# One activation for a gate and its sigmoid, a later place for a tile's split, and a ninth output buffer

## The chip, the cores and the metric

The kernel runs on one core of one Trainium2 chip. The time is device microseconds of one execution. The median of three runs of the kernel before is 1108.38 us (1107.98 to 1109.35).

## The reference

Attention with a sigmoid in place of a softmax feeds a gated layer with RMS norm, whose output feeds a second block that has no nonlinearity of its own. All is float32.

```
scores = q @ k.T / sqrt(64) - log(448)            # 4 batches, 12 heads, 448 tokens
x      = sigmoid(scores) @ v                      # 1792 tokens x 768
xn     = x / sqrt(mean(x*x) + 1e-6) * rms_g
g      = xn @ w_gate                              # 768 -> 1536
val    = xn @ w_val
y      = (g * sigmoid(g) * val) @ w_out           # 1536 -> 768
out    = ((y @ w1) * (y @ w2)) @ w3 @ w_out2      # 768 -> 1024 -> 768
```

## The kernel before

Everything is kept transposed: features on the 128 partitions, the 448 tokens of a batch along the row. A matmul in full precision is made of three fast ones (`mm3`, L296 to L298): each operand is split into a rounded high part and the rest. For weights the split is made by ScalarE or GpSimd (high part, L126 or L128) and GpSimd (rest, L129); for activations by `split2`: ScalarE writes the high part (L312), VectorE the rest (L315). Weights arrive as pairs of 32-bit words and VectorE builds float32 of them in five operations (`to_float`, L106 to L119). So VectorE works as a decoder of weights through the first quarter of the kernel, and its other work stands in the same queue between the decoding steps.

The program runs in stages. First comes attention for batches 0 and 1: twelve `visit`s, one for each pair of heads. In a visit TensorE makes the scores of one pair (L377, L389) and the product with v of the pair before (`attend`, L403, L407), and ScalarE copies that product out of its one accumulator buffer (`take_out`, L427) into a tile `xr`. These tiles are few (`A1`, `xr=8`); a tile comes free when `load_x` (L469, VectorE) has multiplied it by the norm's factor, which for batch 0 can happen only after that batch's norm (L445 to L456). Beside the last visits `split_x` makes the operands of the next stage.

Then come three pairs of `w3o_group`s (w3 times w_out2, L339 to L341, copied out at L343), with the norm and the splits of batch 1 between them on VectorE, and then the gated layer for batches 0 and 1: for each of twelve tiles m and each batch b a gate group and a value group of 18 fast matmuls each (`a_group`). For m below 6 a pair of `w3o_group`s follows each m up to m = 4; from m = 6 on the attention of batches 2 and 3 runs beside the gated tiles, a visit at a time. The second product (`b_group`) follows, and then the same work for batches 2 and 3, where each seven products replace eight (`winograd`, `a_winograd`). The last third is the second block.

In `a_group` the gate's accumulator is read twice: by the sigmoid on ScalarE (L591) and by the product with it on VectorE (L592). The value's accumulator is read by VectorE (L596), and then comes the split of the finished tile (L312, L315). Accumulators `psm` are three in a ring, shared by the gated groups, the w3 groups, the norm and half of the scores. For batch 1 and m below 6 the two accumulators of the attention scores (`sc`) are used, under the name `psa`.

A scheduler lays out each engine's queue from the program; each engine works through its queue in order, so an instruction that waits holds up all behind it.

Of the kernel before, what the change touches and what calls it, by code (L numbers as in the profile page):

```python
# [11 lines left out]
AF = mybir.ActivationFunctionType  # L12
ALU = mybir.AluOpType
# [6 lines left out]
KF1 = FF1 // P  # L20
# [23 lines left out]
def fused_kernel(ctx: ExitStack, tc: tile.TileContext, qkv, wg, wv, wo, w1, w2, w3, wo2, gam, out):  # L44
    nc = tc.nc

    def pool(name, side=None, space=None):
        kw = {}
        if side:
            kw["side"] = side  # L50
        if space is not None:
            kw["space"] = space
        return tc.alloc_tile_pool(name=name, bufs=1, **kw)
# [29 lines left out]
    def scratch(name):  # L83
        return scr.tile([P, S], F32, tag="s", bufs=6, name=name)
# [215 lines left out]
    def accumulate(tiles, xts, ps=None):  # L300
        ps = psm()[:, :S] if ps is None else ps
        n = len(xts)
        j = 0
        for t, kt in tiles:
            for kw in range(kt):
                mm3(ps, t, kw, xts[j], j == 0, j == n - 1)
                j += 1
        return ps

    def split2(dst, src, scalar=True):  # L310
        if scalar:
            nc.scalar.activation(dst[:, 0, :], src, AF.Copy)  # L312
        else:
            nc.gpsimd.tensor_copy(out=dst[:, 0, :], in_=src)
        nc.vector.tensor_tensor(out=dst[:, 1, :], in0=src, in1=dst[:, 0, :], op=ALU.subtract)  # L315
# [30 lines left out]

    A1 = dict(raw=3, a=5, al=2, xr=8, wd=2)
    A2 = dict(raw=2, a=3, al=2, xr=2)  # L350
    att = {"bufs": A1, "pool": pool("att1", "left")}

# [3 lines left out]
    raw, probs, av, acc = {}, {}, {}, {}  # L356
# [119 lines left out]
    def split_x(b, k):  # L476

        if k < KD:
            ready.append(load_x(b, k))
        if k:  # L480
            t = acts["x", b, k - 1] = x_tile("x", b)
            split2(t, ready.pop(0), b == 1)
# [7 lines left out]
    def right_blocks(k, b11, b12, b21, b22):  # L490

        tt = nc.vector.tensor_tensor

        def put(j, bl, src):
            t = acts["w", j, k] = right_tile(f"w{j}", bl)
            split2(t, src)

        t1 = scratch("t1")
        put(0, 0, b11)
        tt(out=t1, in0=b12, in1=b11, op=ALU.subtract)  # L500
        put(5, 1, t1)
        put(2, 0, b21)
        tt(out=t1, in0=b22, in1=t1, op=ALU.subtract)
        put(1, 2, t1)
        tt(out=b12, in0=b22, in1=b12, op=ALU.subtract)
        put(3, 2, b12)
        tt(out=b21, in0=b21, in1=t1, op=ALU.subtract)
        put(4, 2, b21)
        put(6, 1, b22)
# [47 lines left out]
    def a_winograd(m):  # L557
        def done(b, g, v):
            s = scratch("s")
            nc.scalar.activation(s, g, AF.Sigmoid)  # L560
            nc.vector.tensor_tensor(out=s, in0=g, in1=s, op=ALU.mult)
            nc.vector.tensor_tensor(out=s, in0=s, in1=v, op=ALU.mult)  # L562
            acts["h", b, m] = t = h_tile("hm", m)
            split2(t, s)

        winograd(i_a2, m, done)
# [10 lines left out]
    def h_tile(name, m):  # L577
        return pools[f"h{int(m >= KF1 // 2)}"].tile([P, 2, S], F32R, tag="h", bufs=KF1, name=name)
# [3 lines left out]
    def a_group(m, b, which):  # L582
        t = W.get(i_a[m][which])
        ps = None
        if b and m < KF1 // 2:

            ps = ps_sc.tile([P, 2, 512], F32, tag="sc", bufs=2, name="psa")[:, 0, :S]
        ps = accumulate([(t, 6)], [acts["x", b, k] for k in range(KD)], ps)
        if which == 0:
            s = scratch("s")  # L590
            nc.scalar.activation(s, ps, AF.Sigmoid)  # L591
            nc.vector.tensor_tensor(out=s, in0=ps, in1=s, op=ALU.mult)  # L592
            half[m, b] = s
        else:
            s = half.pop((m, b))
            nc.vector.tensor_tensor(out=s, in0=ps, in1=s, op=ALU.mult)  # L596
            t = h_tile("hm", m)
            split2(t, s)
            acts["h", b, m] = t

    def b_group(g, m, b):
        t = [(W.get(i), 6) for i in (i_b2 if g else i_b)[m]]
        ps = accumulate(t, [acts["h", b, k] for k in range(KF1)])
        y = scratch("yf")
        nc.scalar.activation(y, ps, AF.Copy)
        d = yd[g, b, m] = dram.tile([P, S], F32, name=f"y{g}{b}{m}")
        nc.sync.dma_start(out=d, in_=y)
# [8 lines left out]
    def a_units():  # L616
        for m in range(KF1):
            for b in range(2):
                for which in range(2):
                    yield 3.4, (lambda m=m, b=b, w=which: a_group(m, b, w)), i_a[m][which]  # L620

    def b_units(g):
        for m in range(KD):
            for b in range(2):
                yield 6.8, (lambda m=m, b=b: b_group(g, m, b)), (i_b2 if g else i_b)[m][1]
# [62 lines left out]
    a = list(a_units())  # L688
# [118 lines left out]
```

## Time and profile before

| | |
|---|---|
| median of 3 runs | 1108.38 us (1107.98 to 1109.35) |
| profiled execution, its own time | 1100.06 us |
| its span, from the first to the last instruction | 1098.0 us |
| TensorE matmul busy | 1078.6 us (98%) |
| VectorE busy | 801.1 us (73%) |
| ScalarE busy | 387.8 us (35%) |
| GpSimd busy | 476.2 us (43%) |
| mean granted TensorE clock | 0.994 |

PE is TensorE, DVE VectorE, ACT ScalarE, POOL GpSimd. Busy time is summed over the whole span, and so says nothing of a single stage; the rows further down are from single stages.

### The profile page before, as it was taken

To read this page: it belongs to the slowest core of one execution; us is meant where nothing else is said; L and a number is where in the kernel's file an instruction comes from. 1 tells how busy PE (TensorE), PEld (TensorE's weight loads), DVE (VectorE), ACT (ScalarE), POOL (GpSimd) and SP (SyncE) were. 2 spreads that over 40 slices of the span, in tenths; PEclk is the share of its full clock that TensorE was granted. 3 is DMA by queue.
4 is the path that set the end of the run, shared out by engine and by line. 5 is a ranking of instruction groups with operands and counts; after the bars stand their busy time and mean duration, and the time that the engine had idled before them with its cause. 6 is when DMAs were issued, how large, how long until landed. Compare 5 with 4: busy or idle time off the path is not lost.

```text
span 1098.0 us, 14086 instructions
## 1 busy us (share of the span) xinstructions
PE 1078.6 (98%) x5152; PEld 897.2 (82%) x5152; DVE 801.1 (73%) x1054; ACT 387.8 (35%) x707; POOL 476.2 (43%) x382
## 2 busy tenths in 40 slices
PE   9989999998999999999999999999999999999998
PEld 4337899996766676799989898999999999999997
DVE  5988998898446678679889999677787544777500
ACT  5664201111344433214544443133433244333221
POOL 2655443443233323342666554223665424656320
PEclk9989999998999999999999999999999999999999
DMA  7733455557345367653311113666311253210131
GB/s 253 263 131 127 148 172 154 161 194 271 122 158 169 112 244 262 237 214 107 103 59 58 58 58 101 235 248 223 104 59 58 68 166 122 77 58 29 47 100 51
DMA packets 60980, 153.22 MB, mean 140 GB/s; under 512 B 5872, under 2 KB 32624, under 8 KB 60912
## 3 DMA queue, kind: packets, MB, share of 16 engines
q1 hardware_dynamic: 60912, 152.33, 41.2%
q8 instruction: 41, 0.67, 0.2%
q14 instruction: 27, 0.22, 0.1%
HBM read 114.95 MB, written 37.36 MB: 139 GB/s over the span
## 4 chain that ended last, share of the span: by engine, by line
PE 72%; DVE 2%; ACT 1%; DMA 1%; POOL 0%; issue 0%; SPq 0%; DVEq 0%; POOLq 0%; ACTq 0%
PE psm L296 12%; PE psm L297 11%; PE psm L298 11%; PE w L296 10%; PE w L297 10%; PE w L298 10%; PE av L407 3%; PE sc L389 2%; PE psm L377 1%; PE av L403 1%; PE psm L389 1%; DMA wd<-in_wg 1%; DVE s L562 0%; POOL ws L129 0%; ACT a L394 0%; DVE wf L108 0%
## 5 line engine op out<-in xcount | busy, mean ns | idle before, releaser
L296 PE MATMUL w<-w,ws 128*128 128x448 f32 x588 | 216.8, 369 | 1.4 <-DVE c L544 1.1
L297 PE MATMUL w<-w,ws 128*128 128x448 f32 x588 | 216.2, 368 | 0.0
L298 PE MATMUL w<-w,ws 128*128 128x448 f32 x588 | 215.7, 367 | 0.0
L129 POOL TENSOR_TENSOR ws<-wf,ws 128x768 fp32r<-128x768 f32 (+1 forms) x88 | 150.7, 1713 | 139.1 <-ACT ws L126 128.4
L129 POOL TENSOR_TENSOR ws<-wd,ws 128x384 fp32r<-128x384 f32 x112 | 126.8, 1147 | 90.2 <-ACT ws L126 81.3
L129 POOL TENSOR_TENSOR ws<-s,ws 128x384 fp32r<-128x384 f32 x84 | 97.4, 1164 | 78.7 <-ACT ws L126 77.0
L128 POOL CAST ws<-wf 128x768 fp32r<-128x768 f32 (+1 forms) x52 | 47.3, 909 | 181.4 <-DVE wf L119 89.6
L296 PEld LDWEIGHTS w<-w,ws 128*128 128x128 f32 x588 | 110.3, 188 | 14.4 <-issue 3.5
L298 PEld LDWEIGHTS w<-w,ws 128*128 128x128 f32 x588 | 110.4, 188 | 10.8
L297 PEld LDWEIGHTS w<-w,ws 128*128 128x128 f32 x588 | 110.4, 188 | 10.4
L312 ACT ACTIVATE hm<-s 128x448 fp32r<-128x448 f32 x48 | 27.8, 579 | 231.6 <-DVE s L596 174.4
L296 PE MATMUL psm<-hm,ws 128*128 128x448 f32 x288 | 106.6, 370 | 0.0
L297 PE MATMUL psm<-hm,ws 128*128 128x448 f32 x288 | 105.7, 367 | 0.0
L298 PE MATMUL psm<-hm,ws 128*128 128x448 f32 x288 | 105.2, 365 | 0.0
L108 DVE TENSOR_SCALAR wf<-mag 128x768 uint32<-128x768 uint32 (+1 forms) x76 | 66.3, 873 | 36.0 <-POOL ws L129 32.2
L296 PE MATMUL psm<-x,ws 128*128 128x448 f32 x216 | 81.9, 379 | 5.6 <-ACT w3ot L343 2.9
L116 DVE SCALAR_TENSOR_TENSOR wf<-wd,wf 128x768 uint32<-128x768 uint32 (+1 forms) x76 | 85.6, 1126 | 2.3
L119 DVE SCALAR_TENSOR_TENSOR wf<-wd,wf 128x768 uint32<-128x768 uint32 (+1 forms) x76 | 78.9, 1038 | 1.5
L297 PE MATMUL psm<-x,ws 128*128 128x448 f32 x216 | 79.7, 369 | 0.0
L298 PE MATMUL psm<-x,ws 128*128 128x448 f32 x216 | 79.5, 368 | 0.0
L106 DVE TENSOR_SCALAR mag<-wd 128x768 uint32<-128x768 uint32 (+1 forms) x76 | 50.2, 660 | 33.1 <-DMA wd<-in_wo 22.8
L126 ACT ACTIVATE ws<-wd 128x384 fp32r<-128x384 f32 x112 | 54.6, 514 | 46.7 <-PE w L298 38.2
(123 smaller groups left out, 2129.3 us busy)
## 6 DMA issues: line engine op xcount, KB each, us to landing
raw<-in_qkv SPq DMA_DIRECT2D x23, 736.0 KB, 5.5
wd<-in_wo SPq DMA_DIRECT2D x20, 768.0 KB, 5.5
wd<-in_w SPq DMA_DIRECT2D x16, 768.0 KB, 5.0
wd<-w SPq DMA_DIRECT2D x32, 384.0 KB, 3.4
wd<-in_wg SPq DMA_DIRECT2D x12, 768.0 KB, 4.6
wd<-in_wv SPq DMA_DIRECT2D x12, 768.0 KB, 4.7
wd<-in_w SPq DMA_DIRECT2D x16, 512.0 KB, 4.4
w<-wf SPq DMA_DIRECT2D x16, 384.0 KB, 2.6
```

The costliest lines, as they stand in the source:

```text
L106: nc.vector.tensor_scalar(out=mag.bitcast(U32), in0=hi, scalar1=0x7FFFFFFF, scalar2=None, op0=ALU.bitwise_and)
L108: nc.vector.tensor_scalar(out=u, in0=mag.bitcast(U32), scalar1=3, scalar2=0x3FFFFFFF, op0=ALU.logical_shift_left, op1=ALU.bitwise_and,)
L116: nc.vector.scalar_tensor_tensor(out=u, in0=hi, scalar=0xC0000000, in1=u, op0=ALU.bitwise_and, op1=ALU.bitwise_or)
L119: nc.vector.scalar_tensor_tensor(out=u, in0=lo, scalar=29, in1=u, op0=ALU.logical_shift_right, op1=ALU.bitwise_or)
L126: nc.scalar.activation(t[:, 0, :w], f[:, :w], AF.Copy)
L128: nc.gpsimd.tensor_copy(out=t[:, 0, :w], in_=f[:, :w])
L129: nc.gpsimd.tensor_tensor(out=t[:, 1, :w], in0=f[:, :w], in1=t[:, 0, :w], op=ALU.subtract)
L296: nc.tensor.matmul(ps, wl, xt[:, 0, :], start=first, stop=False)
L297: nc.tensor.matmul(ps, wh, xt[:, 1, :], start=False, stop=False)
L298: nc.tensor.matmul(ps, wh, xt[:, 0, :], start=False, stop=last)
L389: nc.tensor.matmul(ps[j], r[d, k], r[d, Q0 : Q0 + S], start=True, stop=True)
L407: nc.tensor.matmul(av[p][d, :], r[:, v + j * D : v + (j + 1) * D], a[:, j, :], start=False, stop=(c == 2))
```

## The change

Three things change. In `a_winograd`, and in `a_group` for m below 6, one activation (`Silu`) computes the gate times its sigmoid; the product on VectorE falls away there, and in `a_group` the gate's accumulator has then one reader. In `a_group` the split of a finished tile is not queued at once: it is kept in a list and queued behind the next gate's activation (or at the start of the next `b_group`), and `keep_in_program_order` holds its ScalarE half at that place in the queue. And the first attention stage has nine `xr` tiles in place of eight.

```
     def split2(dst, src, scalar=True, pin=False):
         if scalar:
-            nc.scalar.activation(dst[:, 0, :], src, AF.Copy)
+            i = nc.scalar.activation(dst[:, 0, :], src, AF.Copy)
+            if pin:
+                tc.keep_in_program_order(i)
...
-    A1 = dict(raw=3, a=5, al=2, xr=8, wd=2)
+    A1 = dict(raw=3, a=5, al=2, xr=9, wd=2)
...
             s = scratch("s")
-            nc.scalar.activation(s, g, AF.Sigmoid)
-            nc.vector.tensor_tensor(out=s, in0=g, in1=s, op=ALU.mult)
+            nc.scalar.activation(s, g, AF.Silu)
             nc.vector.tensor_tensor(out=s, in0=s, in1=v, op=ALU.mult)
...
             s = scratch("s")
-            nc.scalar.activation(s, ps, AF.Sigmoid)
-            nc.vector.tensor_tensor(out=s, in0=ps, in1=s, op=ALU.mult)
+            alone = m < KF1 // 2
+            nc.scalar.activation(s, ps, AF.Silu if alone else AF.Sigmoid)
+            gated()
+            if not alone:
+                nc.vector.tensor_tensor(out=s, in0=ps, in1=s, op=ALU.mult)
             half[m, b] = s
         else:
             s = half.pop((m, b))
             nc.vector.tensor_tensor(out=s, in0=ps, in1=s, op=ALU.mult)
             t = h_tile("hm", m)
-            split2(t, s)
+            unsplit.append((t, s))
             acts["h", b, m] = t
 
+    unsplit = []
+    def gated():
+        if unsplit:
+            split2(*unsplit.pop(0), pin=True)
+
     def b_group(g, m, b):
+        gated()
```

What stands in the queues moves at the gated tiles. TensorE's queue and GpSimd's are the same in both programs, SyncE's has a store and a neighbouring load swapped at a few places, and up to the first gated tile ScalarE's and VectorE's are too, the ninth `xr` tile included: it moves no instruction. The program's lines shift by two to five (before L591, L592, L596, L312, L315, L343; after L594, L597, L601, L312, L317, L345).

The first place is ScalarE's queue at the first gated tiles. Before, from the table load for the first gate on (`s` are the gates, `hm` the high parts of the finished tiles, `w3ot` the copies of the w3 groups):

```order
L591 ACT_TABLE_LOAD
L591 ACTIVATE s_1085<-psm_1066 128x448
L312 ACTIVATE hm_1108<-s_1085 128x448
L591 ACTIVATE s_1130<-psa_1111 128x448
L312 ACTIVATE hm_1153<-s_1130 128x448
L343 ACTIVATE w3ot_1193<-psm_1156 128x384
L343 ACTIVATE w3ot_1247<-psm_1222 128x384
L591 ACTIVATE s_1281<-psm_1262 128x448
```

The same place in the changed program:

```order
L594 ACT_TABLE_LOAD
L594 ACTIVATE s_1085<-psm_1066 128x448
L594 ACTIVATE s_1127<-psa_1108 128x448
L312 ACTIVATE hm_1107<-s_1085 128x448
L345 ACTIVATE w3ot_1189<-psm_1152 128x384
L345 ACTIVATE w3ot_1243<-psm_1218 128x384
L594 ACTIVATE s_1277<-psm_1258 128x448
L312 ACTIVATE hm_1151<-s_1127 128x448
```

The second tile's split (`hm_1151`) now stands behind the copies of the w3 groups and behind the next gate; before, it (`hm_1153`) stood ahead of both.

The second place is VectorE's queue at the end of m = 5, from the split of tile (5, 0) to that of (5, 1). Before (`psa_2092` is the gate of batch 1, `psa_2114` its value):

```order
L315 TENSOR_TENSOR hm_2089<-s_2066,hm_2089 128x448
L106 TENSOR_SCALAR mag_2382<-wd_2217 128x768
L592 TENSOR_TENSOR s_2111<-psa_2092,s_2111 128x448
L107 TENSOR_SCALAR mag_2382<-mag_2382 128x768
L108 TENSOR_SCALAR wf_2383<-mag_2382 128x768
L116 SCALAR_TENSOR_TENSOR wf_2383<-wd_2217,wf_2383 128x768
L119 SCALAR_TENSOR_TENSOR wf_2383<-wd_2217,wf_2383 128x768
L596 TENSOR_TENSOR s_2111<-psa_2114,s_2111 128x448
```

After, where `psa_2102` is that value:

```order
L106 TENSOR_SCALAR mag_2368<-wd_2203 128x768
L107 TENSOR_SCALAR mag_2368<-mag_2368 128x768
L317 TENSOR_TENSOR hm_2078<-s_2054,hm_2078 128x448
L108 TENSOR_SCALAR wf_2369<-mag_2368 128x768
L116 SCALAR_TENSOR_TENSOR wf_2369<-wd_2203,wf_2369 128x768
L119 SCALAR_TENSOR_TENSOR wf_2369<-wd_2203,wf_2369 128x768
L601 TENSOR_TENSOR s_2098<-psa_2102,s_2098 128x448
```

The value's product keeps its place behind the same decoding; the gate's product is gone.

The third place is ScalarE's queue where the attention of batches 2 and 3 begins (`a` and `al` are its sigmoids). Before:

```order
L591 ACTIVATE s_2169<-psm_2150 128x448
L312 ACTIVATE hm_2205<-s_2169 128x448
L394 ACTIVATE a_2219<-sc_2220,bias_s_88 128x896
L394 ACTIVATE a_2224<-sc_2225,bias_s_88 128x896
L591 ACTIVATE s_2248<-psm_2229 128x448
L392 ACTIVATE a_2251<-psm_2252,bias_s_88 128x448
L392 ACTIVATE a_2251<-psm_2253,bias_s_88 128x448
L312 ACTIVATE hm_2278<-s_2248 128x448
```

After:

```order
L594 ACT_TABLE_LOAD
L594 ACTIVATE s_2155<-psm_2136 128x448
L312 ACTIVATE hm_2122<-s_2098 128x448
L396 ACTIVATE a_2205<-sc_2206,bias_s_88 128x896
L396 ACTIVATE a_2210<-sc_2211,bias_s_88 128x896
L594 ACTIVATE s_2234<-psm_2215 128x448
L312 ACTIVATE hm_2193<-s_2155 128x448
L394 ACTIVATE a_2239<-psm_2240,bias_s_88 128x448
L394 ACTIVATE a_2239<-psm_2241,bias_s_88 128x448
```

A table load has come in, the only one that the changed program has more, since the sigmoid here follows gates computed by the other function. The split ahead of the attention's sigmoids is now that of the tile before (`hm_2122` of tile (5, 1), where `hm_2205` was that of (6, 0)); and a split now also stands ahead of the two single sigmoids.

## Rows read from the trace of the kernel before

**Rows 1.** TensorE's waits: who waited for whom, us in total, times, longest.

```profile
PE av L403 <- ACT xr L427: 3.1, 1, 3.1
PE psm L296 <- ACT w3ot L343: 2.9, 3, 1.3
PE sc L389 <- DVE s L596: 2.6, 1, 2.6
PE psm L296 <- DVE s L592: 2.4, 2, 2.2
PE sc L389 <- issue: 1.3, 1, 1.3
PE w L296 <- DVE c L544: 1.1, 1, 1.1
```

**Rows 2.** TensorE in order of time, two visits: start, duration, idle before and releaser.

```profile
69.72 1.02 PE L377 MATMUL psm<-raw 128*128 128x448 f32 x2
...
80.33 1.77 PE L389 MATMUL sc<-raw 64*128 64x448 f32 x8
...
82.78 1.02 PE L377 MATMUL psm<-raw 128*128 128x448 f32 x2
...
86.89 1.02 PE L389 MATMUL sc<-raw 64*128 64x448 f32 x4
```

**Rows 3.** TensorE by stretches: us, PE busy (instructions), granted clock, DMA share, GB/s.

```profile
73.88:80.33 6.45, 6.45 (x15) 0.51 0.03 13
...
265.55:271.40 5.85, 5.85 (x15) 0.50 0.72 245
...
276.26:675.82 399.56, 399.04 (x1884) 1.00 0.40 137
```

**Rows 4.** ScalarE in order of time, at the late copy and at the splits of batch 1.

```profile
73.29 0.54 ACT L427 ACTIVATE xr<-av 128x448 f32<-128x448 f32 x1 [7.32 <-DVE xs L469]
...
118.88 0.58 ACT L312 ACTIVATE x<-xs 128x448 fp32r<-128x448 f32 x1 [12.13 <-DVE xs L469]
119.36 0.47 ACT L343 ACTIVATE w3ot<-psm 128x384 f32<-128x384 f32 x1
```

**Rows 5.** TensorE in order of time, at the first gated tile.

```profile
119.98 0.44 PE L296 MATMUL psm<-x,ws 128*128 128x448 f32 x1 [1.27 <-ACT w3ot L343]
```

**Rows 6.** VectorE in order of time, from the decoding to batch 1's norm and products.

```profile
106.57 0.55 DVE L107 TENSOR_SCALAR mag<-mag 128x768 f32<-128x768 f32 x1
107.22 0.56 DVE L108 TENSOR_SCALAR wf<-mag 128x768 uint32<-128x768 uint32 x1
...
108.70 2.94 DVE L451 RECIPROCAL r<-t 128x448 f32<-128x448 f32 x1
...
118.17 1.27 DVE L469 SCALAR_TENSOR_TENSOR xs<-xr,g_sb,r 128x448 f32<-128x448 f32 x2
```

**Rows 7.** VectorE's waits from 60 to 120 us.

```profile
DVE x L315 <- POOL x L314: 3.1, 4, 1.5
```

**Rows 8.** GpSimd in order of time, the split of a weight tile in the same stretch.

```profile
108.37 1.09 POOL L128 CAST ws<-wf 128x768 fp32r<-128x768 f32 x1 [3.87 <-PE psm L341]
109.54 1.86 POOL L129 TENSOR_TENSOR ws<-wf,ws 128x768 fp32r<-128x768 f32 x1
```

**Rows 9.** VectorE in order of time, decoding with a weight split on GpSimd beside it.

```profile
246.23 1.06 DVE L107 TENSOR_SCALAR mag<-mag 128x768 f32<-128x768 f32 x1
247.38 2.03 DVE L108 TENSOR_SCALAR wf<-mag 128x768 uint32<-128x768 uint32 x1
```

**Rows 10.** VectorE's groups from 119 to 262 us: busy, mean ns, idle before and releaser.

```profile
L315 DVE TENSOR_TENSOR hm<-s,hm 128x448 fp32r<-128x448 f32 x11 | 10.7, 976 | 5.2 <-ACT hm L312 5.2
...
L592 DVE TENSOR_TENSOR s<-psm,s 128x448 f32<-128x448 f32 x6 | 3.7, 616 | 0.0
```

**Rows 11.** ScalarE's groups: the table loads before a gate (busy, mean ns).

```profile
L591 ACT ACT_TABLE_LOAD x2 | 2.6, 1283 | 0.7 <-PE psm L298 0.7
```

**Rows 12.** ScalarE in order of time, where the second attention begins.

```profile
272.75 0.58 ACT L312 ACTIVATE hm<-s 128x448 fp32r<-128x448 f32 x1 [6.21 <-DVE s L596]
```

More of the change, by code (lines that the diff above doesn't have):

```diff
@@ L308, in accumulate, with split2 @@
         return ps
-    def split2(dst, src, scalar=True):
+    def split2(dst, src, scalar=True, pin=False):
         if scalar:
-            nc.scalar.activation(dst[:, 0, :], src, AF.Copy)
+            i = nc.scalar.activation(dst[:, 0, :], src, AF.Copy)
+            if pin:
+                tc.keep_in_program_order(i)
         else:
```

## The prediction

> **What bounds the kernel now.** I read first where TensorE waits, then its rows in order of time around each wait, then the queues of the engines that it waits for. From 276 to 676 us TensorE is busy 399.04 of 399.56 us [rows 3], and it has the same instructions in the same order in both programs. So the end moves only by what TensorE waits, and by what its clock loses. The list of its waits is short [rows 1], and its larger entries stand at three places.
>
> Place A, at 70 us: TensorE stands 3.1 us for the copy of the attention product [rows 1]. The copy, at 73.29, had itself waited 7.32 us for the product that frees an `xr` tile [rows 4]. After it the granted clock is 0.51 for 6.45 us [rows 3], the lower of the two levels (1.2 of 2.4 GHz). The whole price is read from two visits: from L377 to L389 it is 69.72 to 80.33, 10.61 us, and in the next visit 82.78 to 86.89, 4.11 us [rows 2]. The place costs 6.5 us.
>
> Place B, from 118.7 us, the first gated tiles: three waits for w3 copies, 2.9 us together [rows 1], the first of them 1.27 us, after which the tile starts at 119.98 [rows 5].
>
> Place C, 260 to 276 us, where the second attention begins: 2.6 us for the value's product on VectorE, 1.3 without a named releaser, 2.2 (the longest of the L592 entry) for the gate's product [rows 1]; and a stretch of 5.85 us at clock 0.50 [rows 3], which costs 2.9 us. Together 2.6 + 1.3 + 2.2 + 2.9 = 9.0 us.
>
> Late in the kernel 1.1 us remain in the seven-product stage [rows 1].
>
> **The ninth tile.** Copy number 9 finds a free tile at once. Copy 10 needs the one freed at 73.29 [rows 4]; the next `attend` would end about 6.5 us before its present end near 80.3 [rows 2], at 73.8, just behind it. So A goes, and TensorE comes to the first gated tile at 118.7 - 6.5 = 112.2 instead of 118.7.
>
> What is late next? That tile needs an accumulator that a w3 copy on ScalarE frees, at 119.36; the copy stands behind a split of batch 1, which has waited 12.13 us for VectorE [rows 4]. VectorE comes to that product, at 118.17, through decoding, the reciprocal at 108.70 and the rest of the norm in one queue [rows 6], and TensorE is not ahead of it there. I take two corrections. VectorE waited 3.1 us for GpSimd's splits of batch 0 [rows 7], partly because sums of squares, late through A, stand among them: I take half, 1.6 us earlier (bounds 0 and 3.1). Against it, GpSimd's split of a weight tile at 108.37 had waited 3.87 us for TensorE [rows 8], and now starts as soon as the tile is decoded. In the present trace it ran beside the reciprocal; it moves up under L107 and L108, now 0.55 and 0.56 us [rows 6]. Under such a split the two take 1.06 and 2.03 [rows 9]: 2.0 us later (bounds 0 and 2.0). So the tile starts at 119.98 + 0.4 = 120.4, and TensorE stands 8.2 us in place of 1.27.
>
> The Trainium skill speaks against this part of the change: in SBUF — State Buffer, Who interferes with whom, a GpSimd instruction and certain VectorE ones exclude each other for a whole instruction. By that rule a split of 1.09 + 1.86 us [rows 8] could hold VectorE 2.95 us and not 2.0, and the total below would be -6.3 and not -7.3 us; the reciprocal's 2.94 us beside one [rows 6] agrees with the page's exception for one-input operations.
>
> The clock fell after a stand of 3.1 us at A, so I let it fall here too, for a stretch like A's: 6.45 us at 0.51 is 3.2 us (bounds 0, and both stretches seen, 3.2 + 2.9 = 6.1). At about 130 us TensorE is then 0.4 + 3.2 = 3.6 us later than now, although A is gone.
>
> **The gate's activation and the later split, up to m = 5.** From there TensorE bounds. VectorE loses 12 products of 0.616 us (six on `psm` with a row, six on `psa` alike), 7.4 us, and about half of the 5.2 us that its splits wait for ScalarE [rows 10], 2.6: some 10 us of 143, so it falls no further behind. The remaining waits of B, 2.9 - 1.27 = 1.6 us, and the 0.2 beside the 2.2 for the gate's product [rows 1], come from w3 copies held by a split on ScalarE and from L592; the first order fence shows the split moved behind them. What stands behind a pinned split in ScalarE's queue is there the next gate's activation, and the split itself is wanted only by the second product, after m = 11. I take all, 1.8 us (bounds 0 and 1.8). TensorE is 1.8 us late at C.
>
> **C.** The gate on `psa` is read by ScalarE alone, so the 1.3 us wait goes. The value's product stands behind the same decoding as before (second fence) but VectorE has 10 us less ahead of it and needs only 2.6. The 2.2 us came from the gate's activation behind a split that waited 6.21 us for VectorE [rows 12]; that split is now an older tile's (third fence). An m = 6 gate still needs VectorE, so I leave 0.5 us. With these stands gone the clock has no reason to fall: 9.0 - 0.5 = 8.5 us gained (bounds 3.9, the 1.3 and 2.6 alone, and 9.0).
>
> **What costs nothing.** One more table load, 1.28 us [rows 11], falls to the m = 6 gate on ScalarE, whose accumulator is wanted again only three groups later; without that cover it would cost its 1.28. SyncE issues a store and a neighbouring load in the other order at a few places; no wait of TensorE [rows 1] is for either. Products of the second gated stage: 24 fall away from VectorE, which TensorE awaits there for 1.1 us only; I take 0.6 (bounds 0 and 1.1).
>
> **Sum.** + 0.4 (start of the first tile) + 3.2 (clock) - 1.8 - 8.5 - 0.6 = -7.3 us. The profiled execution, 1100.06 us (span 1098.0 and 2.1 around it), becomes 1092.8. The runs' median is 8.3 us above that execution; I take the difference over unchanged: 1108.38 - 7.3 = 1101.1 us. Least and most favourable ends of the terms: the start from -3.1 to +2.0, the clock 0 to 6.1, B -1.8 to 0, C -9.0 to -3.9, the last -1.1 to 0: -15.0 to +4.2. They will not all fall together: the forecast's own range is -4 to -11, 1097.4 to 1104.4.
>
> **Rivals.**
> 1. No fall of the clock, or VectorE much earlier at the first tile. For it: no stand in [rows 1] is longer than A's, so what the clock does after 8 us is not shown. Against it: it fell after 3.1. Without the 3.2: -10.5; with the start also 1.6 earlier than now (no GpSimd penalty): -12.5, 1095.9 us.
> 2. C stays, since VectorE's queue is tied to TensorE by the weight tiles and gives its 10 us back as waits. For it: GpSimd's wait of 3.87 us for TensorE [rows 8]. Against it: behind the value's product stands only one tile's decoding. Then 0.4 + 3.2 - 1.8 - 0.6 = +1.2, 1109.6 us: no change.
> 3. Slower: splits pinned ahead of the attention's single sigmoids (third fence) hold ScalarE for VectorE, and the scores reach `attend` late. For it: a split there waited 6.21 us [rows 12]. Against it: it was then the newest tile's, and from 276 us on TensorE waits hardly at all [rows 3]. There are 12 visits; at 0.6 us each the gain is gone, from 0.8 us each, 9.6, it is over 2.2 us slower. At 1.0 us: -7.3 + 12 = +4.7, 1113.1 us.
> 4. The ninth tile does not remove A. For it: the margin of copy 10 is half a microsecond. Then A and B's first wait stay and nothing falls anew: -1.8 - 8.5 - 0.6 = -10.9, 1097.5 us.
>
> **Chances.** The forecast 0.60, rival 1 0.18, rival 4 0.04, rival 2 0.10, rival 3 0.08. Differences within 0.2% (2.2 us) are about what a measurement of this kernel cannot tell from no change. Faster: 0.60 + 0.18 + 0.04 = 0.82. Same: 0.10. Slower: 0.08. The range leaves out rivals 2 and 3 and the far end of rival 1: 1095.5 to 1105.0.
>
> **What the changed profile would show.** Right: no wait of `av` for `xr`; the copy L429 without a wait for L471's product; one wait of 7 to 9 us at the first gated tile, behind a split of batch 1, with a stretch at the lower level after it; no wait for L601 or for `sc` near 260 us, clock 1.00 there. Wrong: a start of the first tile far from 120 us, a second wait at C, or TensorE's waits between 280 and 460 us above 1 us. What would upset the number most is the clock after that long stand, 0 to 6.1 us, and after it C.

## The result, and the profile after

The changed kernel takes 1098.30 us (median, 1097.40 to 1098.96), the kernel before 1108.18 us beside it (1105.84 to 1109.35): a ratio of 0.9917, 95% interval 0.9898 to 0.9936. That is 9.9 us faster. The two profiled executions, however, differ by 2.7 us only (spans 1098.0 and 1095.3), because the one of before that the prediction read was 8 us faster than its own median.

The page of the changed kernel, span and busy time of each engine:

```profile
span 1095.3 us, 14055 instructions
...
PE 1079.1 (99%) x5152; PEld 902.5 (82%) x5152; DVE 777.3 (71%) x1018; ACT 390.8 (36%) x708; POOL 473.0 (43%) x382
```

TensorE's waits in it (who waited for whom, us in total, times, longest), against [rows 1]:

```profile
PE psm L296 <- ACT w3ot L345: 6.3, 1, 6.3
PE psm L447 <- POOL acc L441: 2.2, 1, 2.2
PE psm L296 <- DVE s L597: 1.1, 1, 1.1
...
PE psm L391 <- DVE s L601: 0.9, 1, 0.9
...
PE sc L391 <- DVE s L601: 0.2, 1, 0.2
```

And TensorE by stretches (us, busy and instructions, granted clock, DMA share, GB/s), against [rows 3]:

```profile
70.94:94.90 23.96, 23.96 (x117) 1.00 0.35 110
94.90:97.10 2.20, 0.12 (x1) 1.00 0.86 209
97.10:116.30 19.20, 19.06 (x98) 0.91 0.30 100
116.30:122.81 6.51, 0.17 (x2) 0.68 0.52 165
122.81:128.90 6.09, 6.09 (x16) 0.50 0.62 191
128.90:263.66 134.76, 134.76 (x697) 1.00 0.57 188
...
272.25:279.08 6.83, 6.12 (x16) 0.50 0.32 100
```

The wait of `av` for `xr` at 70 us is gone, and TensorE works through to 94.9 at full clock. Two stands have come in its place: 2.2 us at the second norm's matmul, for a sum of squares on GpSimd, and 6.3 us at the first gated tile. After each the granted clock is at its lower level for a while; that costs 0.09 of 19.2, 1.7 us, and half of 6.09, 3.0 us. From 128.9 to 263.7 TensorE never waits. Where the second attention begins, 2.2 us of waits are left (0.2 + 0.9 + 1.1), and with the last of them the clock falls once more, for half of 6.12, 3.1 us.

TensorE has the same instructions in the same order in all kernels here, so the time between the same two instructions can be set side by side. The marks are, by their starts in [rows 2] and [rows 5] and in TensorE's rows in order of time: 69.72 (scores of a visit), 101.13 (matmul of the second norm), 119.98 (first gated tile), 141.70 (a w3 group), 256.76 (the last gated tile ahead of the second attention), 290.89 (a gated tile behind its beginning), 438.47 (a tile of the second product), 677.31 (a product of the second gated stage's block), and the end. Stretches in us; the second row is another execution of the unchanged kernel (the first experiment).

| | to norm | to first gated tile | to w3 group | first gated stage | C | to 438 | second gated stage | rest |
|---|---|---|---|---|---|---|---|---|
| before | 31.41 | 18.85 | 21.72 | 115.07 | 34.13 | 147.58 | 238.84 | 420.72 |
| before, again | 30.12 | 22.20 | 22.07 | 114.83 | 39.16 | 152.18 | 238.80 | 421.86 |
| after | 27.31 | 25.57 | 23.33 | 112.88 | 31.40 | 148.12 | 236.09 | 420.65 |

### The profile page after: what moved, and what is told of

The parts are those of the page before. It is cut to its first block, busy times and chain, and to the rows that moved or that the text cites. A ratio compares the mean times of both kernels' runs of the same rounds, so it can differ in the third digit from the quotient of the medians.

```text
span 1095.3 us, 14055 instructions
## 1 busy us (share of the span) xinstructions
PE 1079.1 (99%) x5152; PEld 902.5 (82%) x5152; DVE 777.3 (71%) x1018; ACT 390.8 (36%) x708; POOL 473.0 (43%) x382
## 4 chain that ended last, share of the span: by engine, by line
PE 74%; DVE 2%; DMA 1%; ACT 0%; issue 0%; SPq 0%; DVEq 0%; ACTq 0%
PE psm L296 12%; PE psm L297 11%; PE psm L298 11%; PE w L296 11%; PE w L297 11%; PE w L298 11%; PE av L409 3%; PE sc L391 2%; DMA wd<-in_wg 1%; PE psm L379 1%; PE av L405 1%; PE psm L391 1%; DVE mag L107 1%; DVE wf L108 0%; DVE wf L116 0%; DVE wf L119 0%
## 5 line engine op out<-in xcount | busy, mean ns | idle before, releaser
L129 POOL TENSOR_TENSOR ws<-wf,ws 128x768 fp32r<-128x768 f32 (+1 forms) x88 | 155.0, 1763 | 134.9 <-ACT ws L126 130.7
L129 POOL TENSOR_TENSOR ws<-wd,ws 128x384 fp32r<-128x384 f32 x112 | 124.5, 1123 | 106.8 <-ACT ws L126 97.4
L129 POOL TENSOR_TENSOR ws<-s,ws 128x384 fp32r<-128x384 f32 x84 | 95.1, 1140 | 67.3 <-ACT ws L126 67.3
L116 DVE SCALAR_TENSOR_TENSOR wf<-wd,wf 128x768 uint32<-128x768 uint32 (+1 forms) x76 | 89.3, 1175 | 2.4
L296 PE MATMUL psm<-x,ws 128*128 128x448 f32 x216 | 83.1, 385 | 7.5 <-ACT w3ot L345 6.3
L108 DVE TENSOR_SCALAR wf<-mag 128x768 uint32<-128x768 uint32 (+1 forms) x76 | 59.8, 787 | 34.7 <-POOL ws L129 30.7
L106 DVE TENSOR_SCALAR mag<-wd 128x768 uint32<-128x768 uint32 (+1 forms) x76 | 56.2, 740 | 36.6 <-DMA wd<-in_wo 23.4
L297 PE MATMUL psm<-x,ws 128*128 128x448 f32 x216 | 81.2, 376 | 0.0
L298 PE MATMUL psm<-x,ws 128*128 128x448 f32 x216 | 81.0, 375 | 0.0
L296 PE MATMUL psm<-ab,ws 128*128 128x448 f32 x192 | 70.7, 368 | 0.0
```

The lines of the kernel that those rows point to most:

```text
L106: nc.vector.tensor_scalar(out=mag.bitcast(U32), in0=hi, scalar1=0x7FFFFFFF, scalar2=None, op0=ALU.bitwise_and)
L108: nc.vector.tensor_scalar(out=u, in0=mag.bitcast(U32), scalar1=3, scalar2=0x3FFFFFFF, op0=ALU.logical_shift_left, op1=ALU.bitwise_and,)
L116: nc.vector.scalar_tensor_tensor(out=u, in0=hi, scalar=0xC0000000, in1=u, op0=ALU.bitwise_and, op1=ALU.bitwise_or)
L129: nc.gpsimd.tensor_tensor(out=t[:, 1, :w], in0=f[:, :w], in1=t[:, 0, :w], op=ALU.subtract)
L296: nc.tensor.matmul(ps, wl, xt[:, 0, :], start=first, stop=False)
L297: nc.tensor.matmul(ps, wh, xt[:, 1, :], start=False, stop=False)
```

## The experiments

Stretches of the same kind for every kernel run, in us, with the median time and the ratio to before (95% interval):

| | to norm | to first gated | to w3 | first gated stage | C | to 438 | second gated stage | median | ratio |
|---|---|---|---|---|---|---|---|---|---|
| unchanged | 30.1 | 22.2 | 22.1 | 114.8 | 39.2 | 152.2 | 238.8 | 1106.44 | 1.0002 (0.9982–1.0023) |
| ninth tile alone | 26.2 | 25.6 | 22.2 | 115.1 | 35.9 | 152.2 | 238.3 | 1106.94 | 1.0004 (0.9987–1.0022) |
| change without ninth tile | 32.1 | 18.7 | 21.8 | 112.9 | 31.8 | 148.9 | 236.0 | 1097.50 | 0.9915 (0.989–0.9939) |
| one activation alone | 31.6 | 18.7 | 21.7 | 112.9 | 35.1 | 147.7 | 236.1 | 1096.61 | 0.9914 (0.9886–0.9941) |
| later split alone | 31.1 | 18.9 | 21.7 | 113.7 | 33.9 | 150.1 | 239.0 | 1099.73 | 0.9941 (0.9924–0.9958) |
| activation, first stage | 29.5 | 20.4 | 21.8 | 112.9 | 33.8 | 149.3 | 238.7 | 1101.53 | 0.9956 (0.994–0.9972) |
| activation, second stage | 29.7 | 22.4 | 22.0 | 114.9 | 36.0 | 149.5 | 236.4 | 1102.76 | 0.9969 (0.9957–0.9981) |
| change, two decodings held | 27.0 | 25.6 | 22.9 | 112.9 | 25.5 | 149.0 | 236.4 | 1091.80 | 0.9873 (0.9856–0.9891) |
| held, first tile remade | 26.3 | 17.5 | 23.6 | 114.7 | 26.3 | 150.1 | 236.3 | 1086.50 | 0.9836 (0.9821–0.985) |
| held, eight tiles | 31.3 | 19.1 | 21.7 | 112.9 | 25.8 | 149.6 | 236.3 | 1090.52 | 0.9875 (0.9854–0.9895) |
| held, split at once | 27.4 | 25.6 | 23.0 | 112.9 | 25.7 | 150.4 | 235.9 | 1091.36 | 0.9873 (0.9857–0.989) |
| remade, without the activation | 26.5 | 17.5 | 24.5 | 117.0 | 25.6 | 149.6 | 239.4 | 1092.90 | 0.9878 (0.9854–0.9902) |

**The unchanged kernel, again.** No edit.

> The kernel before, unchanged. Both theories: its time stays at its median, about 1108 us, ratio 0.998 to 1.002. What is asked is its second profile: the first one's own time was 1100.06 us, 6 to 9 us below the runs of the same kernel. If the second profile's time is near 1108, the difference lies in the lengths of the stands at 70 us and 260 us and in the stretches at the lower clock, and a comparison of two single profiles is worth no more than those; if it is again near 1100, the difference lies outside what a profile shows.

The medians agree, but its profiled execution took 1113.49 us, 13 us more than the first one. TensorE's waits in it:

```profile
PE psm L296 <- ACT w3ot L343: 5.4, 4, 4.6
PE av L403 <- ACT xr L427: 3.3, 1, 3.3
PE psm L389 <- DVE s L596: 3.0, 1, 3.0
PE psm L377 <- DMA raw<-in_qkv: 2.6, 1, 2.6
PE sc L389 <- DVE s L596: 2.6, 1, 2.6
```

Here the first gated tile waits 4.6 us without a ninth tile, a wait of 3.0 us at C is new against [rows 1], and a load of the attention comes 2.6 us late. So one execution of this kernel is no measure of a change of 10 us. The mean of the two spans, 1104.75 us, plus the 2.1 around a span, is 1106.8 us, at the medians of before. In "why" below I measure against both.

**The ninth tile, alone and left out.** One edit on the kernel before, the opposite one on the changed kernel:

```
-    A1 = dict(raw=3, a=5, al=2, xr=8, wd=2)
+    A1 = dict(raw=3, a=5, al=2, xr=9, wd=2)
```

> The kernel before with nine xr tiles and nothing else. Theory 1 (the ninth tile gives itself back): the stand of 3 us at 70 us goes, one stand of 6 to 8 us comes at the first gated tile with the lower clock behind it, and the place at 260 us stays as it is: -3 to +4 us, ratio 0.997 to 1.004. Theory 2 (the ninth tile is the gain): the 6.5 us of the place at 70 us are kept: -5 to -7 us, ratio 0.994 to 0.9955.

> The changed kernel with eight xr tiles again: one activation and later split alone. Theory 1: the stand at 70 us stays with its stretch at the lower clock, the first gated tile waits 1 to 3 us and no clock falls there, the place at 260 us costs 0 to 6 us in place of 9: -6 to -11 us against the kernel before, as fast as the changed kernel within 3 us. Theory 2: 6.5 us of the changed kernel's gain are lost: -2 to -4 us.

Alone it changes nothing (1.0004), and the change without it is as fast as with it. The reason stands in TensorE's rows of the kernel with the ninth tile alone, at the norm and at the first gated tile:

```profile
96.18 0.64 PE L445 MATMUL psm<-acc,ones 128*128 128x448 f32 x1 [1.15 <-POOL acc L439]
...
121.75 0.71 PE L296 MATMUL psm<-x,ws 128*128 128x448 f32 x1 [7.90 <-ACT w3ot L343]
```

TensorE comes to the norm at 96.18 (101.13 and 100.40 in the two executions of before), after a stand of 1.15 us, and then stands 7.90 us. What it saves at 70 us it gives back before 122: the first two stretches are 51.8 us together, and 52.3 in the unchanged kernel run beside it (50.3 in the first profile).

**One activation alone, and each half of it.** The kernel before, with `Silu` in both places, or only in `a_group` for m below 6, or only in `a_winograd`; the split stays queued at once and the tiles are eight:

```
-            nc.scalar.activation(s, ps, AF.Sigmoid)
-            nc.vector.tensor_tensor(out=s, in0=ps, in1=s, op=ALU.mult)
+            alone = m < KF1 // 2
+            nc.scalar.activation(s, ps, AF.Silu if alone else AF.Sigmoid)
+            if not alone:
+                nc.vector.tensor_tensor(out=s, in0=ps, in1=s, op=ALU.mult)
```

> The kernel before with one activation for gate times sigmoid (both places), but the split queued at once as before, and eight xr tiles. Theory 1 (VectorE's queue is what is late at 260 us): 12 products of 0.62 us less in it are 7.4 us, enough for most of the place: the waits there shrink from 6.1 to 1 to 3 us: -4 to -9 us. Rival: the split that stands at once behind its tile holds ScalarE for VectorE, and this is what is late: -0 to -3 us, and only the later split brings the rest.

> Before, with the one activation in the first gated stage alone (12 visits), split queued at once, eight output tiles. Theory 1 (VectorE comes to the second stage with a shorter queue, and the later waits of the first stage go): nearly the whole gain, 7 to 10 us faster, ratio 0.991 to 0.9935. Rival (each stage pays its own share, and the second stage's stands of 9 us in before go only with the activation there): 2 to 4 us faster, ratio 0.9965 to 0.998.

> Before, with the one activation in the second gated stage alone (4 visits), split queued at once, eight output tiles. Theory 1: VectorE is late by what stands in its queue ahead, which this does not shorten; 4 products less of 0.55 us: 0 to 2.5 us faster, ratio 0.9977 to 1.000. Rival (as for the run beside it): 5 to 8 us faster, ratio 0.993 to 0.9955.

By the medians it alone has the whole gain, 9.8 us, a little more than its theory had. That theory's place was C, however, and there its profile still has 5.1 us of waits where 1 to 3 were expected. Its halves give 4.6 and 3.3 us, and 0.9956 times 0.9969 is 0.9925, inside the interval of both together. Neither theory had the sizes: the first stage is worth less than the theory said, the second more (24 products fall away there, not the four of the expectation). In the table the second half shows in its own stage alone, 238.8 to 236.4; the first half shows in the first gated stage, 114.8 or 115.1 to 112.9. At C it shows less clearly: 33.8 us, where the executions without it have 34.1 to 39.2. So the gated stages account for some 5 of the 9.8 us (2.0 and 2.7). The rest lies in stretches that differ as much between two executions of the unchanged kernel, and no run here places it.

**The later split alone.** Before, with `unsplit` and `gated` of the change, sigmoid and product everywhere, eight tiles:

```
-            split2(t, s)
+            unsplit.append((t, s))
```

> Before, with the later queueing of the split alone (sigmoid and product stay two operations in both stages, eight output tiles). Theory 1 (the gain is VectorE's: 16 products at half width less ahead of the second stage): nothing of that is removed here, so within 1.5 us of before, ratio 0.9985 to 1.0015, with the stand at the first gated tile and the second stage's waits on L591 and L592 as in before. Theory 2 (a good part of the gain is ScalarE's, which is freed of splits ahead of the sigmoid): 3 to 6 us faster, ratio 0.9945 to 0.997.

It is 6.4 us faster, a little more than the second theory had; the theory that the gain is VectorE's alone falls. With the activation in place the same edit adds nothing to the median (0.9915 with it, 0.9914 without). I read the two edits as two ways to relieve one place: the split waits on ScalarE for VectorE's product, and ScalarE's next gate behind it. ScalarE's groups from 126 to 262 us in the changed kernel (busy, mean ns, idle before):

```profile
L312 ACT ACTIVATE hm<-s 128x448 fp32r<-128x448 f32 x11 | 6.3, 574 | 31.8 <-DVE s L601 31.8
...
L594 ACT ACTIVATE s<-psm 128x448 f32<-128x448 f32 x7 | 3.8, 547 | 15.9 <-PE psm L298 15.8
```

In the kernel before the same group of splits held ScalarE 114.4 us in this stretch, here 31.8. In the first gated stage the table fits this reading: 113.7 us with the split alone, 112.9 with the activation, with or without the later split. At C it does not: TensorE waits there 4.7 us with the split alone, 5.1 with the activation alone and 2.9 with both, in one execution of each. So the reading is not shown for the whole kernel. How much of the 6.4 us falls at C and how much elsewhere I can't settle from single executions that scatter as much: its first gated stage is 1.2 to 1.4 us shorter, and its C, 33.9, lies only just below the executions without a change there (34.1, 39.2, 35.9).

**Two decodings held back.** In the changed kernel VectorE's queue at C is this (start, us, line, tiles, idle before):

```profile
263.41 0.62 DVE L601 TENSOR_TENSOR s<-psa,s 128x448 f32<-128x448 f32 x1
263.94 0.55 DVE L106 TENSOR_SCALAR mag<-wd 128x768 uint32<-128x768 uint32 x1
...
269.51 0.77 DVE L106 TENSOR_SCALAR mag<-wd 128x768 uint32<-128x768 uint32 x1 [0.72 <-DMA wd<-in_wg]
270.20 0.61 DVE L601 TENSOR_TENSOR s<-psm,s 128x448 f32<-128x448 f32 x1
270.74 1.63 DVE L107 TENSOR_SCALAR mag<-mag 128x768 f32<-128x768 f32 x1
272.29 0.61 DVE L597 TENSOR_TENSOR s<-psm,s 128x448 f32<-128x448 f32 x1
```

The products that TensorE waits for (263.41, 270.20 and 272.29, each ending as TensorE goes on) stand behind decoding steps, and one of those behind a load. The edit queues two decodings, those of the gate and value weights of m = 8, behind the value's product of tile (5, 1) and the gate's product of tile (6, 1). I call the result the held kernel.

```
+    held = {}
...
-                    f = to_float(f, w)
+                    with tc.issue_after(held[i]) if i in held else ExitStack():
+                        f = to_float(f, w)
...
+                if (m, b) == (KF1 // 2, 1):
+                    held[i_a[m + 2][1]] = i.ins
...
+            if (m, b) == (KF1 // 2 - 1, 1):
+                held[i_a[m + 3][0]] = i.ins
```

> The changed kernel, with the decoding of two weight tiles on VectorE held back until behind the value product of the fifth head's second batch and the gate product of the sixth's. Theory (what the second stage still waits for, 2.2 us, and the 3.1 to 3.4 us that the lower granted clock costs behind it, come from VectorE's decoding ahead of its products): both go, 3 to 6 us below the changed kernel, 1092.5 to 1095.5 us where the changed one is at 1098, ratio to before 0.986 to 0.989. Rival 1 (the decoding only moves, and the convolution's tiles wait for their weights instead): within 1 us of the changed kernel. Rival 2 (TensorE's clock falls later instead, at the next wait): 0 to 2 us below it.

The median falls by 6.5 us to 1091.80, a little more than the theory's 3 to 6. The kernel before was also 2.1 us faster beside this run than beside the changed kernel; against it the gain grows from 9.9 to 14.3 us, by 4.4. The stretch C takes 25.5 us, where it took 31.4; TensorE from 257 to 284 us, in this kernel:

```profile
257.00:284.00 27.00, 26.61 (x123) 1.00 0.49 166
```

No fall of the clock is left here, and none comes later. VectorE now waits for ScalarE there:

```profile
259.40 0.61 DVE L606 TENSOR_TENSOR s<-psa,s 128x448 f32<-128x448 f32 x1
...
264.69 0.62 DVE L606 TENSOR_TENSOR s<-psm,s 128x448 f32<-128x448 f32 x1
268.23 0.62 DVE L600 TENSOR_TENSOR s<-psm,s 128x448 f32<-128x448 f32 x1 [2.91 <-ACT s L597]
```

**The same, with eight tiles, and with the split at once.** Two single edits on the held kernel, each by itself:

```
-    A1 = dict(raw=3, a=5, al=2, xr=9, wd=2)
+    A1 = dict(raw=3, a=5, al=2, xr=8, wd=2)
...
-            unsplit.append((t, s))
+            split2(t, s)
```

> The kernel with the two decodings held back, with eight output tiles in place of nine. Theory (the ninth tile gives back at the norm and at the first gated tile what it takes away at 70 us): within 2 us of the held kernel, 1089.8 to 1093.8 us. Rival (its gain was hidden by the second stage's waits, and shows now that these are gone): 4 to 7 us above it, 1096 to 1099 us.

> The kernel with the two decodings held back and nine output tiles, with the split of a gated tile queued at once as in before. Theory (with the one activation in place the later queueing adds nothing, as between the two runs with and without it): within 2 us of the held kernel, 1089.8 to 1093.8 us. Rival (the split, queued at once, brings a product and a subtraction of VectorE ahead of the held decodings and frees ScalarE late at 260 to 280 us): 2 to 5 us above it.

Both are within 1.3 us of it: neither edit gains a measurable time here, also where C no longer hides what it might bring.

**The first gated tile remade.** On the held kernel: the two later pairs of w3 groups are called ahead of the second batch's splits, so their copies stand ahead of them on ScalarE; the decoding of the second gate weight is queued behind the second norm on VectorE, that of the next two w3 tiles behind the last product of the second batch. One of the calls that split and load weights ahead is left out, so that these come with the next one.

```
             w3o_group(kt, nh)
+            if (kt, nh) == (2, 1):
+                continue
             W.split_to(i_w3[kt][1] + 2 + nh)
...
+    w3o_groups(1)
+    w3o_groups(2)
     for k in range(KD + 1):
-        if k % 3 == 2:
-            w3o_groups(k // 3 + 1)
         split_x(1, k)
...
-        nc.vector.tensor_tensor(out=r, in0=r, in1=t, op=ALU.mult)
+        i = nc.vector.tensor_tensor(out=r, in0=r, in1=t, op=ALU.mult)
+        if b == 1:
+            held[i_a[0][1]] = i.ins
...
+        if (b, k) == (1, KD - 1):
+            held[i_w3[W3_FIRST][0]] = held[i_w3[W3_FIRST][1]] = i.ins
```

> The kernel with the two decodings held back, and place B remade as well: the w3 copies are queued on ScalarE ahead of the second batch's splits, the decoding of the second gate weight stands on VectorE behind the second batch's norm, that of the next two w3 tiles behind the second batch's last product. Theory (the stand of 6.3 us at the first gated tile is that norm, late behind the decoding, and copies behind splits): the stand shrinks to 1.5 us or less and the clock loses less than the 3.4 us or so of now; part comes back at the next tiles, which wait for the weights that were put back: 3 to 8 us below the held kernel, 1084 to 1089 us where that is at 1091.8, ratio to before 0.980 to 0.984. Rival (VectorE's whole queue between 96 and 131 us is full, so any order of it costs TensorE the same): within 2 us of the held kernel, ratio 0.9855 to 0.989.

The median is 1086.50 us, 18.4 below before and the best of all kernels here. TensorE's waits and its stretches from the norm on:

```profile
PE psm L299 <- POOL ws L129: 2.4, 3, 1.1
...
PE psm L450 <- POOL acc L444: 1.2, 1, 1.2
PE psm L344 <- POOL ws L129: 1.2, 1, 1.2
```

```profile
94.49:115.70 21.21, 20.01 (x112) 1.00 0.42 127
115.70:135.00 19.30, 16.92 (x83) 1.00 0.46 149
...
260.00:280.00 20.00, 20.00 (x90) 1.00 0.51 169
```

The first gated tile starts at 114.21 without a wait. As the theory said, part comes back: 3.6 us of waits for the weights that were put back, none longer than 1.2. The clock stays at 1.00 through all of it.

**The same without the activation.** Sigmoid and product in both places, all else as in the kernel just shown.

```
-            alone = m < KF1 // 2
+            alone = False
```

> The kernel with both places remade (nine output tiles, later split, held decodings, the first gated tile's queue), with sigmoid and product in place of the one activation everywhere. Theory (the activation works by a shorter VectorE queue in both places, and the waits that it removes come back without it): 3 to 9 us above the kernel with both places remade, 1089.5 to 1095.5 us where that is at 1086.5, ratio to before 0.986 to 0.9915, with waits on L605 and L611 from 120 to 280 us. Rival (the order on VectorE is all that matters, and the products fit in between): within 1.5 us of it, ratio 0.982 to 0.985.

It is 6.4 us slower than the kernel with the activation (12.4 us faster than the kernel before beside it, where that one is 18.4), so the rival falls. The second gated stage is 3.1 us longer again (239.35 and 236.25), the first 2.3 (117.02 and 114.71). TensorE waits there for the products that are back (L605) and, in the second stage, for sums of its seven products that stand behind such products in VectorE's queue (L551, L553):

```profile
PE w L299 <- DVE c L553: 2.2, 3, 1.1
...
PE psm L299 <- DVE s L605: 1.1, 1, 1.1
PE w L299 <- DVE v L551: 1.0, 3, 0.5
PE psm L344 <- DVE s L605: 0.8, 1, 0.8
```

## Why the prediction was right in its time, and where its steps failed

The median lies 2.8 us below the forecast of 1101.1 us, inside the forecast's own range and the wider one. The signs that the prediction had set are less kind. The wait of `av` is gone and the first gated tile waits behind a split of batch 1, as it said. But that wait is 6.3 us and not 7 to 9, and C has waits and a fall of the clock, which was to be a sign of being wrong. By the stretches of the table, with the forecast's terms put to them:

| | forecast | after, less before | after, less mean of the two |
|---|---|---|---|
| 70 us to C (A, first tile, clock, B) | +1.8 | +2.0 | +1.0 |
| C | -8.5 | -2.7 | -5.2 |
| to 438 us | 0 | +0.5 | -1.8 |
| second gated stage | -0.6 | -2.7 | -2.7 |
| rest, with the start | 0 | +0.1 | -0.7 |
| sum (of unrounded starts) | -7.3 | -2.7 | -9.5 |

That the first row agrees is luck, since two of its three terms miss and cancel. Against the first profile, counted from the first mark, the first tile starts 2.6 us later in place of 0.4 (2.0 at most by the bounds), the clock behind it costs 3.0 in place of 3.2, and B gives 3.6 in place of 1.8 (1.8 at most).

**The ninth tile: right in kind, its start mis-sized.** A went, for about the 6.5 us that were read from the two visits (31.41 to 27.31 us, with 2.2 of the norm's new wait in the latter: 6.3), and what came back is about as much, as forecast. The pieces were sized wrongly. I had VectorE 1.6 us earlier at the second norm, since GpSimd's sums of squares would no longer be late. They were not earlier (the last ends at 97.2 us before and after): it stands on GpSimd behind a split of the first batch, and that behind VectorE.

```profile
89.47 1.34 POOL L441 TENSOR_TENSOR acc<-acc,sq 128x448 f32<-128x448 f32 x1
95.54 0.56 POOL L316 CAST x<-xs 128x448 fp32r<-128x448 f32 x1 [4.72 <-DVE xs L471]
96.06 1.13 POOL L441 TENSOR_TENSOR acc<-acc,sq 128x448 f32<-128x448 f32 x1
```

That is the 2.2 us at the norm, a wait that the forecast did not have, with 1.7 us of clock behind it. The queue was there to be read; I looked only at what A had delayed in it.

**GpSimd's split beside the decoding: right.** I had 2.0 us for it, by [rows 9] against [rows 6]. VectorE after:

```profile
107.49 0.55 DVE L107 TENSOR_SCALAR mag<-mag 128x768 f32<-128x768 f32 x1
108.15 0.99 DVE L108 TENSOR_SCALAR wf<-mag 128x768 uint32<-128x768 uint32 x1
109.17 2.48 DVE L116 SCALAR_TENSOR_TENSOR wf<-wd,wf 128x768 uint32<-128x768 uint32 x1
111.58 2.94 DVE L453 RECIPROCAL r<-t 128x448 f32<-128x448 f32 x1
```

L108 takes 0.99 in place of 0.56 and L116 2.48 in place of the 0.96 that the same step took at 107.82 in the first profile: 1.95 us more, one step later than I had put it. GpSimd's split beside them:

```profile
107.70 1.02 POOL L128 CAST ws<-wf 128x768 fp32r<-128x768 f32 x1 [2.28 <-DVE wf L119]
108.80 2.04 POOL L129 TENSOR_TENSOR ws<-wf,ws 128x768 fp32r<-128x768 f32 x1
```

When L108 started, 0.57 us of the cast were left, and 1.67 of the subtraction when L116 did, 2.24 together. The whole split, 3.06 us here, would have been too high a price; the row was nearer. By the Trainium skill, SBUF — State Buffer, Who interferes with whom, of a GpSimd instruction and certain VectorE ones whichever starts first blocks the other for the whole instruction; its exception for VectorE instructions with one input does not hold in the two-port modes, which the prediction left out. These rows do not speak against that: VectorE lost 1.95 us beside 2.24 that were left, and L108, with one input, was lengthened too. The first tile started at 122.81, not 120.4: the 1.6 that did not come, and 0.8 more. The unchanged kernel's second execution has the same 0.99 and 2.49, and its tile starts at 122.60; so this term is not the change's alone.

**The clock after the first tile: right.** 3.2 us forecast, 3.0 measured. **B: gone, as forecast, and worth twice as much.** No wait is left from 128.9 to 263.7 us. To the w3 group 1.4 us are gained beside the clock's cost, where 1.0 was forecast; but the w3 wait that goes there (1.0 at 124.9) goes with the late first tile and not with the moved split, since the change without the ninth tile still has it (1.0 at 125.6). The first gated stage is 2.2 us shorter where 0.8 of the forecast's 1.8 lay there. Its waits were 1.0; the rest lies in TensorE's busy time (114.06 and 112.89 us), and why is not shown.

**C: the failed step.** "VectorE has 10 us less ahead of it and needs only 2.6", and "With these stands gone the clock has no reason to fall". VectorE's products before, to set beside those at 263.41, 270.20 and 272.29 above (the value's of tiles (5, 1) and (6, 0), the gate's of (6, 1)):

```profile
264.88 0.61 DVE L596 TENSOR_TENSOR s<-psa,s 128x448 f32<-128x448 f32 x1
...
272.10 0.62 DVE L596 TENSOR_TENSOR s<-psm,s 128x448 f32<-128x448 f32 x1
...
275.58 0.62 DVE L592 TENSOR_TENSOR s<-psm,s 128x448 f32<-128x448 f32 x1 [1.12 <-ACT s L591]
```

Counted from the start of C (256.76 before, 259.02 after) they come 3.7, 4.2 and 5.5 us earlier, not 10. That was nearly enough for the first, whose wait fell from 2.6 to 0.2 us. But with that wait and the 1.3 gone TensorE also comes sooner to the other two, which still stand behind decoding, once behind a decoding step that waited for its load. They were 0.9 and 1.1 us late, and with the last the clock fell, for 3.1 us. Of the 5.8 us that C gave less than forecast (2.7 for 8.5), 1.7 are waits (2.2 for 0.5) and 3.1 the clock; about 1 lies in TensorE's busy time and stays open. Holding back two decodings moves rows of VectorE, and on SyncE one load past another transfer. It took C to 25.5 us, about what the forecast would have left of it (34.13 - 8.5 = 25.6), and 4.4 to 6.5 us from the time: that their place in the queue is the cause of what was left at C is shown.

Why VectorE gained 4 to 6 us there and not 10 is read from one execution each, and not shown by a run. From 126 to 262 us it was busy 124.90 us before and 125.45 after, although the products (7.4 us) had left. Three of its groups in that stretch after (busy, mean ns, idle before):

```profile
L317 DVE TENSOR_TENSOR hm<-s,hm 128x448 fp32r<-128x448 f32 x11 | 13.9, 1260 | 2.0 <-ACT hm L312 1.9
...
L106 DVE TENSOR_SCALAR mag<-wd 128x768 uint32<-128x768 uint32 x15 | 10.9, 727 | 5.3 <-DMA wd<-in_wg 2.9 <-DMA wd<-in_wv 2.4
...
L317 DVE TENSOR_TENSOR x<-xs,x 128x448 fp32r<-128x448 f32 x4 | 2.4, 612 | 0.0
```

The eleven subtractions of the gated tiles take 13.9 us where they took 10.7 [rows 10], moved as they are to other neighbours; the second batch's products and subtractions, late through the first tile, bring 2.5 us more into the stretch; and the decoding waits 5.3 us for loads, 2.8 before. Rival 2 (C stays) was partly right in what came out, and its reason is not shown.

**The second gated stage: mis-sized.** 2.7 us in place of 0.6. I took TensorE's 1.1 us from one entry of the list of its waits; there was one more of 0.3. With those too short for the list TensorE's waits fall by 1.5 us there; the other 1.2 lie in its busy time (237.31 and 236.07 us), and why is not shown. That the activation is the cause is: the run with it there alone has 2.4 us less in this stretch, and its other stretches lie within what the unchanged kernel and the ninth tile alone show, or near it.

**The level.** I took over 8.3 us between the first profile and the median "unchanged". That was the luckiest step. The second execution of the unchanged kernel is 13.5 us longer than the first, and 3.4 of them lie at the first tile, 5.0 at C and 4.6 up to 438 us, where a load comes late; the change acts at the first two and not on the third. Against the mean of the two executions the sum is -9.5, beside -9.9 of the medians. So the forecast came near because C was forecast too large against one execution, and that execution had less to lose at C than the others without a change there (34.1 us, for 35.9 and 39.2). Rivals 1, 3 and 4 are out: the clock did fall, TensorE waited from 276 to 676 us no more than before, and A went.

## What to carry to other kernels

Time taken off an engine with a long queue reaches the instruction that is waited for only in part, and a wait that is removed brings the waiting engine sooner to the next one; what is waited for must also be queued ahead of what can wait. A buffer that removes one stand moves the next engine's queue into its place: follow each queue past it, GpSimd's too, before counting the gain. And profile the unchanged kernel twice before pricing a change of 1%.

## What the runs showed of the hardware

Which step a split on GpSimd overlaps is decided by under a microsecond, and in two executions of the same kernel it moved the first gated tile by 2.6 us. In the first profile GpSimd's split started at 108.37, when VectorE was nearly through its decoding step (L116, 107.82 to 108.78), and it ran beside the reciprocal, which took 2.94 us, as it does after the change with no split beside it; in the second execution it started at 107.65, under L108 and L116 (it waits for TensorE, which came to the norm 0.7 us earlier there), and VectorE was 2.6 us later at the reciprocal (111.34 for 108.70; 0.7 of it was there before), TensorE as much at the first gated tile.

The clock did not fall after every wait. At the norm it fell after a wait of 2.2 us, to the lower of its two levels (1.2 of 2.4 GHz); after 1.2 us at the same place in the remade kernel, and after its four waits of 0.4 to 1.2 us from 117 to 146 us, it stayed at 1.00. Nor did it fall after 1.4 us at the norm and single waits of up to 1.7 us behind it in that kernel without the activation. In the change without the ninth tile it fell at C (at 268.7 us) behind two waits of 0.9 us, the second ended at 267.9; in the held kernel with eight tiles it did not after one of 0.7 us there. The length of one wait does not settle it here: after 1.9 us at the norm in the held kernel it fell, after 2.1 us for a load at 425 us in that kernel with the split at once it did not.

`Silu` costs ScalarE about what the sigmoid did: 547 ns on `psm` for 546 before, 544 on `psa` for 528 (means from 126 to 262 us).
